# Squared-ReLU attention and an h-swish MLP in one kernel: the order of the loads in the first chunk, the queue of the weight loads, and the pace of the MLP's first units

## The chip, the cores and the metric

One core of one Trainium2 chip runs the whole kernel. The metric is the device time of one execution in microseconds, median of several runs; lower is better. A profiled execution gives the trace that is read below.

## The reference

`u`, `v` have shape 4 x 3008 x 256, `z` has 4 x 3008 x 64, all fp32. `w_in` (256 x 2048) and `w_out` (2048 x 256) arrive as float64.

```python
scores = (1.0 / S) * np.matmul(z, z.transpose(0, 2, 1))
attn = np.maximum(scores, 0.0) ** 2
x = (u * np.matmul(attn, v)).reshape(B * S, D)
h = x @ w_in
g = h * np.clip(h + 3.0, 0.0, 6.0) / 6.0
y = g @ w_out
```

## The kernel before

**Precision.** TensorE works on a rounded fp32 format (`F32R`). Each operand is split in a high part (rounded copy) and a low part (raw minus high, on VectorE), and a product is three matmuls: low x high, high x low, high x high. The scores need two, because `zx` and `zy` hold high and low of z stacked on the 128 partitions.

**Tiling.** The 24 chunks `(b, c)` are 512 rows of one batch entry b (the sixth of each has 448). For each chunk the attention walks 12 pairs p of 128 keys each: `scores(b, c, p)` makes 4 matmuls into PSUM, ScalarE takes the ReLU (`rt`), squares it into the rounded `ah` and once more into `r`, VectorE subtracts to get `al`; `attend(b, c, p)` then makes 12 matmuls of `ah`, `al` with `vh`, `vl`. The score matrix is symmetric: a pair computed in one chunk is written to DRAM (`keep`, tile `d`, two DMAs) and fetched again for its mirror in a later chunk (`fetch_mirrored`, tile `l`, four DMAs), where VectorE transposes it (`turn`, tile `rm`) and splits it (`from_mirror`); such a mirrored pair needs no score matmuls. The step number g counts the 288 pairs; scores are made two pairs ahead of `attend` for g < 28, one ahead later.

**First chunk.** At step p of chunk 0 (`i == 0`) the program also splits the next pair of v (`split_v(0, p + 1)`) and on even p a z piece (`split_z(0, p // 2 + 2)`): everything of batch entry 0 is loaded and split while its first chunk runs. Score pair p needs z piece p // 2. Before, v is loaded twice: raw by SP's queue, and rounded (`vh`) by GpSimd's queue; z pieces 2 to 5 are also loaded twice.

**MLP.** It trails the attention: for each chunk 16 units, `up(q)` (12 matmuls into `h`, then ScalarE and VectorE make `gh`, `gl`) and `down(q)` (12 matmuls into `y`). `mlp_units` emits as many units after each step as a target asks, from step FIRST = 28 on.

**Weights.** The float64 weights come in 16 pieces of 512 KB (`wraw`). `weight_ops` is a generator that turns them into fp32 high and low parts with 8 VectorE instructions each (`split64` six, `finish64` two) and one ScalarE copy; `weight_work(n)` emits the next n of these 128 instructions. Its first call only fetches two pieces; each later piece is fetched after the sixth instruction of the piece two before it. Unit n of the first MLP chunk needs piece n, and `weight_needed` emits what is missing on the spot.

**Buffers.** The pool `rpool` has 5 buffers with one tag, shared by `rt`, `r`, `rm`, `y` and `wraw` (two pieces of which are held while weights are under work). Each engine works through its instructions in program order, and so does each DMA queue's issuing engine: SP for most loads and stores, GpSimd (POOL) for the loads that round.

Of the kernel before, what the change touches and what calls it, by code (L numbers as in the profile page):

```python
# [13 lines left out]
B, S, D, DQK, DFF = 4, 3008, 256, 64, 2048  # L14
NT = B * S
P = 128
CH = 512
NCH = 6
NJ = 24
NPAIR = NJ // 2  # L20
# [2 lines left out]
NFP = NF // 2  # L23

FIRST = 28

TINY = 1.125 * 2.0 ** -15

# [2 lines left out]
def relu2_attention_then_hswish_mlp(  # L31
# [22 lines left out]
    nc = tc.nc  # L54
# [14 lines left out]
    def f(ap):  # L69
        return ap.bitcast(F32)  # L70
# [4 lines left out]
    def split(hi, lo, raw, rounded=False):  # L75
        if not rounded:
            nc.scalar.copy(out=hi, in_=raw)  # L77
        nc.vector.tensor_tensor(out=lo, in0=raw, in1=f(hi), op=ALU.subtract)  # L78
# [69 lines left out]
    def fetch_w(kind, q):  # L148
        _, _, src, cols = w_piece(kind, q)
        if wide:  # L150
            raw = rpool.tile([P, 2, D, 2], U32, tag="r", name="wraw")
            nc.sync.dma_start(
                out=raw.rearrange("p k n w -> p k (n w)"),
                in_=src[:, :, 2 * cols.start:2 * cols.stop],
            )
        else:
            raw = rpool.tile([P, 2, D], F32, tag="r", name="wraw")
            nc.sync.dma_start(out=raw, in_=src[:, :, cols])
        raws["w", kind, q] = raw

    raws = {}
# [3 lines left out]
    def fetch_v(b, p):  # L165

        if b == 0 and p < NPAIR - 1:
            raw = vpool.tile([P, 2, D], F32, tag="vl", name="vraw")
        else:
            raw = stg.tile([P, 2, D], F32, tag="stg", name="vraw")  # L170
        vh = vpool.tile([P, 2, D], F32R, tag="vh", name="vh")
        vt[b, p] = vh
        raws["v", p] = raw
        j0 = p * 2 * P
        for dst, queue in ((raw, nc.sync), (vh, nc.gpsimd))[:1 if b else 2]:
            if p < NPAIR - 1:
                queue.dma_start(
                    out=dst, in_=v[b, j0:j0 + 2 * P, :].rearrange("(r q) d -> q r d", q=P)
                )
            else:  # L180
                queue.dma_start(out=dst[:, 0, :], in_=v[b, j0:j0 + P, :])
                for h in range(2):
                    queue.dma_start(out=dst[64 * h:64 * h + 64, 1, :], in_=v[b, j0 + P:S, :])

    def split_v(b, p):
        vh, raw = vt[b, p], raws.pop(("v", p))
        vl = vpool.tile([P, 2, D], F32R, tag="vl", name="vl")
        split(vh, vl, raw, rounded=b == 0)
        vt[b, p] = (vh, vl)

    def fetch_z(b, k):
        if b == 0:
            raw = xpool.tile([P, CH], F32, tag=("xh0", "xh1", "xl0", "xl1")[k % 4], name="zraw")
        else:
            raw = stg.tile([P, CH], F32, tag="stg", name="zraw")
        zx = zpool.tile([P, CH], F32R, tag="zx", name="zx")
        zy = zpool.tile([P, CH], F32R, tag="zy", name="zy")
        zt[b, k] = (zx, zy)
        raws["z", k] = raw
        cols = slice(k * CH, (k + 1) * CH)  # L200
        nc.sync.dma_start(out=raw, in_=zz[b, :, cols])
        if b == 0 and k > 1:
            nc.gpsimd.dma_start(out=zx[0:64], in_=zz[b, 0:64, cols])
            nc.gpsimd.dma_start(out=zy[64:128], in_=zz[b, 64:128, cols])
# [33 lines left out]
    def fetch_mirrored():  # L238

        while to_fetch and len(mirrored) < 2:  # L240
            b, c, p = to_fetch[0]
            if (b, p // 2, c) not in whole:
                return
            fetch_pair(*to_fetch.pop(0))
# [33 lines left out]
    def turn(b, c, p):  # L278

        if p // 2 >= c:  # L280
            return
        n = width(c)
        t = mirrored.pop((b, c, p))
        rn = rpool.tile([P, 2, CH], F32, tag="r", name="rm")[:, :, :n]
        nc.vector.transpose(  # L285
            out=rn.rearrange("p r (k e) -> p r k e", e=32),
            in_=t[:, :n // 32].rearrange("p k (r e) -> p r k e", r=2),
        )
        turned[b, c, p] = rn
        fetch_mirrored()  # L290

    def from_mirror(b, c, p):
        n = width(c)
# [74 lines left out]
    def width(c):  # L368
        return CH if c < NCH - 1 else S - CH * (NCH - 1)
# [23 lines left out]
    def load_u(b, c):  # L393
        n = width(c)
        t0 = b * S + c * CH
        t = upool.tile([P, 2, CH], F32, tag="u", name="u")
        nc.sync.dma_start(
            out=t[:, :, :n], in_=ut[:, t0:t0 + n].rearrange("(k p) t -> p k t", p=P)
        )
        raw_x[b, c] = t  # L400
# [69 lines left out]
    chunks = [(b, c) for b in range(B) for c in range(NCH)]  # L470
    pairs = [(b, c, p) for b, c in chunks for p in pairs_of(c)]
# [4 lines left out]
    NU = len(units)  # L476
# [57 lines left out]
    def weight_work(n):  # L534
        for _ in range(n):
            next(w_ops, None)
# [17 lines left out]
    def maybe_split():  # L554

        if to_split and to_split[0] < avs[0]:
            i = to_split.pop(0)
            split_x(*chunks[i])
            if i + 2 < len(chunks):
                load_u(*chunks[i + 2])  # L560
# [9 lines left out]
    def turn_next():  # L570

        while g_turned[0] < min(g_done + 1, len(pairs)):
            turn(*pairs[g_turned[0]])
            g_turned[0] += 1

    with tc.manual_schedule():
        nc.vector.memset(three, 3.0)
        fetch_z(0, 0)
        fetch_v(0, 0)
        split_z(0, 0)  # L580
        fetch_z(0, 1)
        fetch_v(0, 1)
        weight_work(1)
        split_v(0, 0)
        split_z(0, 1)
        scores(0, 0, 0)
        fetch_z(0, 2)
        fetch_v(0, 2)
        scores(0, 0, 1)
        fetch_v(0, 3)  # L590
        g_done = 2
        to_fetch += [(b, c, p) for b, c, p in pairs if p // 2 < c]
        g_turned = [2]
        for i, (b, c) in enumerate(chunks):
            ahead = b + 1 if c == NCH - 1 and b + 1 < B else None
            for p in range(NPAIR):
                g = i * NPAIR + p
                pair = pairs[g]
                lead = 2 if g < FIRST else 1
                if i == 0:  # L600
                    if p + 1 < NPAIR:
                        split_v(0, p + 1)
                    if p % 2 == 0 and p // 2 + 2 < NCH:
                        split_z(0, p // 2 + 2)
                while g_done < min(g + lead + 1, len(pairs)):
                    scores(*pairs[g_done], square_on_act=i < 3)
                    g_done += 1
                if p > 3:
                    fetch_mirrored()
                if p < NPAIR - 1:  # L610
                    turn_next()
                if i == 0:
                    if p + 4 < NPAIR:
                        fetch_v(0, p + 4)
                    if p % 2 == 0 and p // 2 + 3 < NCH:
                        fetch_z(0, p // 2 + 3)
                    if p == 6:
                        load_u(*chunks[0])
                        load_u(*chunks[1])
                maybe_split()  # L620
                if g >= FIRST:
                    weight_work(5)
                elif p < NPAIR - 2:
                    weight_work(4 if i else 2)
                if ahead and p < NPAIR - 1:
                    if p:
                        split_v(ahead, p - 1)
                    if p < NPAIR - 2:
                        fetch_v(ahead, p)
                    if p % 2 == 1:  # L630
                        fetch_z(ahead, p // 2)
                    elif p:
                        split_z(ahead, p // 2 - 1)
                elif b and c == 0 and p < 4:
                    if p in (1, 2):
                        split_v(b, NPAIR - 3 + p)
                    if p < 2:
                        fetch_v(b, NPAIR - 2 + p)
                    if p == 2:
                        fetch_z(b, NCH - 1)  # L640
                    if p == 3:
                        split_z(b, NCH - 1)
                attend(*pair)
                turn_next()
                if p == NPAIR - 1:
                    avs[0] += 1
                total = len(pairs) - FIRST
                target = max(0, g + 1 - FIRST) * ((len(chunks) - 1) * NU - 4) // total
                mlp_units(target - units_done[0])
        mlp_units(1)  # L650
        maybe_split()
        mlp_units(len(chunks) * NU - units_done[0])
# [35 lines left out]
```

## Time and profile before

| | |
|---|---|
| median of 3 runs | 1992.83 us (1990.3 to 1993.12) |
| profiled execution, its own time | 1995.22 us |
| its span, first to last instruction | 1993.4 us |
| TensorE busy / VectorE / ScalarE / GpSimd | 1957.0 / 1278.8 / 987.6 / 14.2 us |
| granted TensorE clock, mean | 0.995 |
| matmuls | 8688 |

How to read it: busy TensorE time is the sum of stretches in which a matmul is in flight, so it does not tell apart a matmul at 2.4 GHz and one at 1.2 GHz; start-to-start distances and the granted clock do. PE is TensorE, PEld its weight loads, DVE VectorE, ACT ScalarE, POOL GpSimd, SP the queue engine. Times in the rows are microseconds from the span's start.

### The profile page before, as it was taken

How to read it: one execution, taken by the hardware profiler on the slowest of the kernel's cores; microseconds unless marked ns; L12 is line 12 of the kernel's file. 1: busy time of each engine (PE TensorE's matmuls, PEld its weight loads, DVE VectorE, ACT ScalarE, POOL GpSimd, SP SyncE). 2: the span in 40 equal slices, each digit the busy share in tenths (PEclk: the TensorE clock that was granted, in tenths of full speed). 3: DMA queues.
4: the chain of work that ended last, by engine and by line, in shares of the span. 5: the costliest groups of instructions: out<-in, count | busy, mean ns of one | idle time of the engine just before them, and what ended most of it. 6: DMA issues, size and time to landing. Idle time of an engine off the chain costs nothing.

```text
span 1993.4 us, 22057 instructions
## 1 busy us (share of the span) xinstructions
PE 1957.0 (98%) x8688; PEld 1634.6 (82%) x8688; DVE 1278.8 (64%) x1276; ACT 987.6 (50%) x1058; POOL 14.2 (1%) x26
## 2 busy tenths in 40 slices
PE   7899999999999999999999999999999999999999
PEld 5778788788888888888888888888888888888888
DVE  5798665676556666577655665657756555666654
ACT  6665444455544444456554454444554444444343
POOL 2000000000000000000000000000000000000000
PEclk9899999999999999999999999999999999999999
DMA  9753432525232233252323233334342323333300
GB/s 262 209 158 93 93 64 72 129 57 127 61 84 71 63 91 85 61 130 79 102 68 102 51 82 74 83 70 112 87 117 57 96 48 87 74 82 71 94 10 21
DMA packets 403272, 178.15 MB, mean 89 GB/s; under 512 B 250080, under 2 KB 385248, under 8 KB 403168
## 3 DMA queue, kind: packets, MB, share of 16 engines
q1 hardware_dynamic: 399232, 172.55, 34.3%
q0 software_dynamic: 3936, 4.20, 0.9%
q8 instruction: 68, 1.11, 0.2%
q14 instruction: 36, 0.29, 0.1%
HBM read 104.07 MB, written 72.61 MB: 89 GB/s over the span
## 4 chain that ended last, share of the span: by engine, by line
PE 88%; DVE 5%; ACT 2%; DMA 2%; issue 1%; SPq 1%; DVEq 0%; ACTq 0%
PE o L73 33%; PE h L73 24%; PE y L73 24%; PE s L73 7%; DMA zraw<-in_zz_dram 1%; DMA vraw<-in_v_dram 1%; DVE rt L436 1%; DVE al L354 1%; ACT rt L435 1%; DVE gl L78 1%; DVE al L301 1%; DVE rm L285 1%; ACT gh L77 0%; ACT rt L334 0%; ACT r L344 0%
## 5 line engine op out<-in xcount | busy, mean ns | idle before, releaser
L436 DVE SCALAR_TENSOR_TENSOR rt<-rt,h 128x1024 f32<-128x1024 f32 (+1 forms) x192 | 230.0, 1198 | 425.3 <-ACT rt L435 425.0
L435 ACT ACTIVATE rt<-h,three 128x1024 f32<-128x1024 f32 (+1 forms) x192 | 211.0, 1099 | 547.8 <-PE h L73 534.4
L73 PE MATMUL o<-ah,vl 128*128 128x512 f32 (+1 forms) x1152 | 447.3, 388 | 7.9 <-DVE u L405 2.7
L73 PE MATMUL o<-ah,vh 128*128 128x512 f32 (+1 forms) x1152 | 446.1, 387 | 0.0
L73 PE MATMUL o<-al,vh 128*128 128x512 f32 (+1 forms) x1104 | 429.2, 389 | 8.0 <-DVE al L301 5.8
L73 PE MATMUL y<-gh,w_out_l 128*128 128x512 f32 (+1 forms) x768 | 296.1, 386 | 1.6 <-DVE w_out_l L133 1.6
L73 PE MATMUL y<-gl,w_out_h 128*128 128x512 f32 (+1 forms) x768 | 296.4, 386 | 1.0 <-DVE gl L78 1.0
L73 PE MATMUL h<-xh,w_in_l 128*128 128x512 f32 (+1 forms) x768 | 295.9, 385 | 0.0
L73 PE MATMUL y<-gh,w_out_h 128*128 128x512 f32 (+1 forms) x768 | 295.9, 385 | 0.0
L73 PE MATMUL h<-xl,w_in_h 128*128 128x512 f32 (+1 forms) x768 | 295.9, 385 | 0.0
L73 PE MATMUL h<-xh,w_in_h 128*128 128x512 f32 (+1 forms) x768 | 295.9, 385 | 0.0
L78 DVE TENSOR_TENSOR gl<-rt,gh 128x1024 fp32r<-128x1024 f32 (+1 forms) x192 | 230.7, 1201 | 80.4 <-ACT gh L77 77.8
L73 PEld LDWEIGHTS o<-ah,vl 128*128 128x128 f32 x1152 | 217.6, 189 | 54.4 <-issue 4.5
L77 ACT CAST gh<-rt 128x1024 fp32r<-128x1024 f32 (+1 forms) x192 | 197.2, 1027 | 121.0 <-DVE rt L436 121.0
L73 PEld LDWEIGHTS o<-al,vh 128*128 128x128 f32 x1104 | 208.8, 189 | 52.1 <-DVE al L301 9.0
L73 PEld LDWEIGHTS o<-ah,vh 128*128 128x128 f32 x1152 | 217.8, 189 | 40.6
L334 ACT ACTIVATE rt<-s 128x1024 f32<-128x1024 f32 x168 | 171.2, 1019 | 115.5 <-PE s L73 108.9
L346 DVE TENSOR_TENSOR r<-rt 128x1024 f32<-128x1024 f32 (+1 forms) x139 | 168.8, 1214 | 87.0 <-ACT rt L334 86.8
L354 DVE TENSOR_TENSOR al<-r,ah 128x1024 fp32r<-128x1024 f32 (+1 forms) x139 | 169.7, 1221 | 18.5 <-ACT r L344 5.6
L301 DVE TENSOR_TENSOR al<-rm,ah 128x1024 fp32r<-128x1024 f32 (+1 forms) x120 | 141.2, 1176 | 42.4 <-ACT ah L299 42.3
L73 PEld LDWEIGHTS y<-gh,w_out_l 128*128 128x128 f32 x768 | 144.3, 188 | 29.3 <-DVE w_out_l L133 1.3
L73 PEld LDWEIGHTS y<-gl,w_out_h 128*128 128x128 f32 x768 | 144.2, 188 | 29.2 <-DVE gl L78 2.4
(51 smaller groups left out, 1809.5 us busy)
## 6 DMA issues: line engine op xcount, KB each, us to landing
d<-r SPq DMA_DIRECT2D x220, 256.0 KB, 2.9
l<-d SPq DMA_DIRECT2D x320, 128.0 KB, 3.2
l<-d SPq DMA_DIRECT2D x160, 112.0 KB, 2.9
vraw<-in_v_dram SPq DMA_DIRECT2D x44, 256.0 KB, 3.5
u<-in_ut_dram SPq DMA_DIRECT2D x20, 512.0 KB, 4.2
out_dram<-y SPq DMA_DIRECT2D x40, 256.0 KB, 3.5
zraw<-in_zz_dram SPq DMA_DIRECT2D x24, 256.0 KB, 3.8
wraw<-in_w_in_dram SPq DMA_DIRECT2D x8, 512.0 KB, 5.0
```

The lines of the kernel that those rows point to most:

```text
L73: nc.tensor.matmul(out, lhsT=lhsT, rhs=rhs, start=start, stop=stop)
L77: nc.scalar.copy(out=hi, in_=raw)
L78: nc.vector.tensor_tensor(out=lo, in0=raw, in1=f(hi), op=ALU.subtract)
L285: nc.vector.transpose(out=rn.rearrange("p r (k e) -> p r k e", e=32), in_=t[:, :n // 32].rearrange("p k (r e) -> p r k e", r=2),)
L301: nc.vector.tensor_tensor(out=al[:, :, :n], in0=rn, in1=f(ah[:, :, :n]), op=ALU.subtract)
L334: nc.scalar.activation(out=rn, in_=s[:, :, :n], func=AF.Relu, scale=1.0 / S)
L346: nc.vector.tensor_tensor(out=r2_of, in0=r_of, in1=r_of, op=ALU.mult)
L354: nc.vector.tensor_tensor(out=l_of, in0=r2_of, in1=h_of, op=ALU.subtract)
L435: nc.scalar.activation(out=rn, in_=h, func=AF.Relu, bias=three)
L436: nc.vector.scalar_tensor_tensor(out=rn, in0=rn, scalar=6.0, in1=h, op0=ALU.min, op1=ALU.mult)
```

## The change

Five edits. (1) The start loads z pieces 0 to 3 and v pairs 0 to 3 first; the first two weight pieces are no longer fetched there. In the loop, the loads of step p come at its beginning. (2) v of batch entry 0 is loaded once, raw; the rounded copy `vh` is made by ScalarE in `split_v`. (3) Weight pieces are fetched through GpSimd's queue, and weight work begins at step p = 5 of chunk 0. (4) Mirrored pairs are first fetched at p = 10 of chunk 0 (before: p = 4), and `u` at p = 7 (before: 6). (5) Weight instructions per step are 2 for p = 5 to 11 of chunk 0 (before: 2 for p = 0 to 9); then 4 in a step whose newest scores are direct and 2 (3 from g = 28) in one whose newest pair is mirrored (before: 4 in steps 0 to 9 of a chunk, 5 from g = 28); and the first SLOW = 16 units are emitted one per step (before: 364 units spread evenly over 260 steps, 1.4 each); the rest then run at 348 / 244 = 1.43 per step.

```diff
@@ fetch_w
-            nc.sync.dma_start(
+            nc.gpsimd.dma_start(
                 out=raw.rearrange("p k n w -> p k (n w)"),
...
@@ fetch_v
-        for dst, queue in ((raw, nc.sync), (vh, nc.gpsimd))[:1 if b else 2]:
...
+        if p < NPAIR - 1:
+            nc.sync.dma_start(
+                out=raw, in_=v[b, j0:j0 + 2 * P, :].rearrange("(r q) d -> q r d", q=P)
+            )
...
@@ split_v
-        split(vh, vl, raw, rounded=b == 0)
+        split(vh, vl, raw)
@@ before the loop
         fetch_z(0, 1)
         fetch_v(0, 1)
-        weight_work(1)
+        fetch_z(0, 2)
+        fetch_z(0, 3)
+        fetch_v(0, 2)
+        fetch_v(0, 3)
         split_v(0, 0)
         split_z(0, 1)
         scores(0, 0, 0)
-        fetch_z(0, 2)
-        fetch_v(0, 2)
         scores(0, 0, 1)
-        fetch_v(0, 3)
@@ in the loop
                 if i == 0:
+                    if p + 4 < NPAIR:
+                        fetch_v(0, p + 4)
+                    if p < 2:
+                        fetch_z(0, p + 4)
...
-                if p > 3:
+                if i or p > 9:
                     fetch_mirrored()
                 if p < NPAIR - 1:
                     turn_next()
+                if i == 0 and p == 7:
+                    load_u(*chunks[0])
+                    load_u(*chunks[1])
+                maybe_split()
                 if i == 0:
-                    if p + 4 < NPAIR:
-                        fetch_v(0, p + 4)
-                    if p % 2 == 0 and p // 2 + 3 < NCH:
-                        fetch_z(0, p // 2 + 3)
-                    if p == 6:
-                        load_u(*chunks[0])
-                        load_u(*chunks[1])
-                maybe_split()
-                if g >= FIRST:
-                    weight_work(5)
-                elif p < NPAIR - 2:
-                    weight_work(4 if i else 2)
+                    weight_work(2 if p > 4 else 0)
+                elif is_mirrored(*pairs[g_done - 1]):
+                    weight_work(3 if g >= FIRST else 2)
+                else:
+                    weight_work(4)
...
-                total = len(pairs) - FIRST
-                target = max(0, g + 1 - FIRST) * ((len(chunks) - 1) * NU - 4) // total
+                target = g + 1 - FIRST
+                if target > SLOW:
+                    all_but = (len(chunks) - 1) * NU - 4 - SLOW
+                    target = SLOW + (target - SLOW) * all_but // (len(pairs) - FIRST - SLOW)
                 mlp_units(target - units_done[0])
```

`is_mirrored(b, c, p)` returns `p // 2 < c`.

## Rows read from the trace of the kernel before

**Rows 1.** The page: busy time of the engines (us, share of the span, instructions), and the granted TensorE clock in 40 slices of 50 us.

```profile
PE 1957.0 (98%) x8688; PEld 1634.6 (82%) x8688; DVE 1278.8 (64%) x1276; ACT 987.6 (50%) x1058; POOL 14.2 (1%) x26
...
PEclk9899999999999999999999999999999999999999
```

**Rows 2.** What TensorE waited for in the first 260 us: total us, times, longest.

```profile
PE s L73 <- issue: 8.1, 2, 4.3
PE s L73 <- DVE zx L78: 6.4, 2, 6.1
PE o L73 <- DVE al L301: 3.6, 4, 1.4
PE o L73 <- DVE al L354: 2.2, 4, 0.9
PE y L73 <- DVE w_out_l L133: 1.6, 2, 0.9
```

**Rows 3.** Timeline of TensorE: the matmuls at which it had been idle in the two large gaps (start, duration, what, idle before).

```profile
30.52 0.47 PE L73 MATMUL s<-zy,zx 128*128 128x512 f32 x1 [3.82 <-issue]
33.49 0.77 PE L73 MATMUL o<-ah,vl 128*128 128x512 f32 x1 [1.49 <-DVE vl L78]
...
53.71 0.77 PE L73 MATMUL s<-zy,zx 128*128 128x512 f32 x1 [4.25 <-issue]
56.94 0.77 PE L73 MATMUL o<-ah,vl 128*128 128x512 f32 x1 [1.18 <-ACT rt L334]
```

**Rows 4.** The chain that ended last, 0 to 70 us: start, us, what.

```profile
17.87 11.06 DMA zraw<-in_zz_dram
...
33.49 5.08 PE o L73 x12
38.58 0.91 PE s L73 x4
39.49 2.72 PE o L73 x12
...
53.71 2.06 PE s L73 x4
...
56.94 5.28 PE o L73 x12
```

**Rows 5.** Timeline of SP's queue and of VectorE around the two gaps.

```profile
38.98 7.71 SPq L254 DMA_DIRECT2D l<-d  x8
...
47.27 0.47 SPq L201 DMA_DIRECT2D zraw<-in_zz_dram  x1
...
29.02 0.68 DVE L78 TENSOR_TENSOR zy<-zraw,zx 64x512 fp32r<-64x512 f32 x1 [6.24 <-DMA zraw<-in_zz_dram]
...
52.21 0.68 DVE L78 TENSOR_TENSOR zy<-zraw,zx 64x512 fp32r<-64x512 f32 x1 [6.69 <-DMA zraw<-in_zz_dram]
```

**Rows 6.** Stretches of 10 us: busy us (instructions) of each engine, granted TensorE clock, DMA share, GB/s.

```profile
20.00:30.00 10.00, 6.63 (x29) 5.18 (x28) 3.69 (x6) 3.66 (x4) 3.62 (x6) 1.00 1.25 342
30.00:40.00 10.00, 7.99 (x23) 5.92 (x24) 8.40 (x12) 6.42 (x7) 0.00 (x0) 0.66 0.70 189
50.00:60.00 10.00, 5.10 (x11) 3.68 (x12) 7.66 (x11) 4.09 (x4) 0.00 (x0) 0.58 1.08 358
```

**Rows 7.** DMA issues of the first 70 us: what, count, KB each, median us from issue to landing.

```profile
d<-r SPq DMA_DIRECT2D x19, 256.0 KB, 5.4
vraw<-in_v_dram SPq DMA_DIRECT2D x11, 256.0 KB, 5.6
vh<-in_v_dram POOLq DMA_DIRECT2D x11, 256.0 KB, 8.3
wraw<-in_w_in_dram SPq DMA_DIRECT2D x3, 512.0 KB, 9.7
```

**Rows 8.** The tile `wraw`, 0 to 250 us (16 pieces): landing times of its DMAs.

```profile
DMA to landing us min/median/max: 4.0/4.8/11.2
```

**Rows 9.** Timeline of ScalarE, one step of chunk 0 and a copy of 128x512.

```profile
33.71 1.04 ACT L344 ACTIVATE r<-rt 128x1024 f32<-128x1024 f32 x1
34.66 1.00 ACT L334 ACTIVATE rt<-s 128x1024 f32<-128x1024 f32 x1
35.69 1.06 ACT L343 ACTIVATE ah<-rt 128x1024 fp32r<-128x1024 f32 x1
...
27.47 0.60 ACT L117 CAST w_in_h<-t 128x512 fp32r<-128x512 f32 x1
```

**Rows 10.** VectorE's groups in the first 250 us, by shape: busy us, mean ns of one. Of the eight instructions of a weight piece the first and the last are shown (L101 to L133: 128 in all).

```profile
L354 DVE TENSOR_TENSOR al<-r,ah 128x1024 fp32r<-128x1024 f32 x26 | 31.8, 1223 | 6.3 <-ACT r L344 5.6
L285 DVE STREAM_TRANSPOSE rm<-l 128x1024 f32<-128x1024 f32 x12 | 14.9, 1238 | 0.0
L436 DVE SCALAR_TENSOR_TENSOR rt<-rt,h 128x1024 f32<-128x1024 f32 x12 | 14.5, 1212 | 5.8 <-ACT rt L435 5.8
L101 DVE TENSOR_SCALAR t<-wraw 128x512 uint32<-128x512 uint32 x16 | 6.7, 421 | 0.0
...
L133 DVE TENSOR_TENSOR w_in_l<-t,w_in_l 128x512 fp32r<-128x512 f32 x8 | 5.5, 691 | 0.2
```

**Rows 11.** Timeline of GpSimd and VectorE: a GpSimd DMA issue while VectorE is in a two-input instruction, and one just after it had waited.

```profile
11.58 0.73 POOL L177 DMA_DIRECT2D vh<-in_v_dram  x1 [0.16 <-issue]
...
11.44 1.23 DVE L354 TENSOR_TENSOR al<-r,ah 128x1024 fp32r<-128x1024 f32 x1
```

More of the change, by code (lines that the diff above doesn't have):

```diff
@@ L25 @@
 FIRST = 28
+SLOW = 16
 TINY = 1.125 * 2.0 ** -15
@@ L157, in fetch_w @@
             raw = rpool.tile([P, 2, D], F32, tag="r", name="wraw")
-            nc.sync.dma_start(out=raw, in_=src[:, :, cols])
+            nc.gpsimd.dma_start(out=raw, in_=src[:, :, cols])
         raws["w", kind, q] = raw
@@ L174, in fetch_v @@
         j0 = p * 2 * P
-        for dst, queue in ((raw, nc.sync), (vh, nc.gpsimd))[:1 if b else 2]:
[L176 to L183, printed above, removed]
+        if p < NPAIR - 1:
[3 more added lines that the diff above has]
+        else:
+            nc.sync.dma_start(out=raw[:, 0, :], in_=v[b, j0:j0 + P, :])
+            for h in range(2):
+                nc.sync.dma_start(out=raw[64 * h:64 * h + 64, 1, :], in_=v[b, j0 + P:S, :])
     def split_v(b, p):
@@ L290, in turn, with is_mirrored @@
         fetch_mirrored()
+    def is_mirrored(b, c, p):
+        return p // 2 < c
     def from_mirror(b, c, p):
@@ L611, in relu2_attention_then_hswish_mlp @@
                     turn_next()
+                if i == 0 and p == 7:
+                    load_u(*chunks[0])
+                    load_u(*chunks[1])
+                maybe_split()
                 if i == 0:
-                    if p + 4 < NPAIR:
-                        fetch_v(0, p + 4)
-                    if p % 2 == 0 and p // 2 + 3 < NCH:
-                        fetch_z(0, p // 2 + 3)
-                    if p == 6:
-                        load_u(*chunks[0])
-                        load_u(*chunks[1])
-                maybe_split()
-                if g >= FIRST:
-                    weight_work(5)
-                elif p < NPAIR - 2:
-                    weight_work(4 if i else 2)
+                    weight_work(2 if p > 4 else 0)
+                elif is_mirrored(*pairs[g_done - 1]):
+                    weight_work(3 if g >= FIRST else 2)
+                else:
+                    weight_work(4)
                 if ahead and p < NPAIR - 1:
```

## The prediction

> **What bounds the kernel now.** I read the page first, then TensorE's waits, the timeline at its two largest gaps, the chain that ended last, and VectorE's and ScalarE's groups. The page says that TensorE is the bound: 1957.0 of 1993.4 us busy, the clock full but for the second slice [rows 1]. No change that leaves the 8688 matmuls as they are can win more than TensorE's idle and slow-clock time, so I add up where that lies. In the first 260 us it waits some 25 us; the largest items are two waits for `s` put down to "issue" (8.1 us), the start itself (nearly all of the 6.4 behind `zx`), `al` (3.6 and 2.2) and `w_out_l` (1.6) [rows 2]. The change touches only this stretch; beyond it the code that is emitted is the same with the MLP a few units later.
>
> The two waits for `s` are the z pieces 4 and 5. TensorE stands still for 3.82 us before 30.52 and 4.25 us before 53.71 [rows 3], and VectorE, which splits z, had stood still for 6.24 and 6.69 us until `zraw` landed, at 29.02 and 52.21 [rows 5]. The first load took 11.06 us [rows 4] while the DMA engines moved 342 GB/s [rows 6]; the second was issued only at 47.27, because SP had spent 7.71 us from 38.98 on eight `l` fetches [rows 5]. So one is late by traffic and one by its place in SP's queue.
>
> What a gap costs is more than its idle time. After each the granted clock falls, to 0.66 in 30 to 40 us and 0.58 in 50 to 60 us [rows 6], that is for part of these stretches at the lower level of 1.2 GHz. Twelve `o` matmuls take 2.72 us at full clock, but 5.08 and 5.28 after the gaps; four `s` take 0.91, and 2.06 after the second [rows 4].
>
> **Part 1: z and v first.** Idle: 3.82 + 1.49 + 4.25 + 1.18 = 10.74 us [rows 3]. Slow clock: (5.08 - 2.72) + (5.28 - 2.72) + (2.06 - 0.91) = 6.1 us, and four `s` after the first gap, priced like those of the second, 1.1 more: 7.2 [rows 4]. Together 17.9 us to win. Unstalled, a step of chunk 0 is 16 matmuls of 0.227 us (2.72 / 12), 3.63 us; step 0 begins when `al` of pair 0 is there, at 11.44 + 1.23 = 12.7 us [rows 11], so step 4 near 27, step 5 near 31, step 7 near 38. Afterwards z pieces 4 and 5 are asked for in steps 0 and 1 and split in steps 4 and 6: some 15 us of room against landings of 5.4 to 11.06 us [rows 4, 7]. GpSimd's queue, which carried twelve loads of `vh` at 8.3 us each [rows 7], then holds only z at the start. The `l` fetch moves to step 10, behind the last z and v. I take the whole 17.9; below it the bound is 9 (one gap replaced by a new one), above it 18.5, since the first z and v loads meet less traffic too (at most some 0.6 us of the start).
>
> **Part 2: `vh` by ScalarE.** One copy of 128x512 takes 0.60 us. A step's `ah`, `r`, `rt` follow each other at some 1 us: 1.00 + 1.06 + 1.04 = 3.10 at most [rows 9]. So ScalarE needs 3.70 us per step against TensorE's 3.63, and 0.15 more from step 5 with one weight copy in four steps. Over twelve steps that is 0.07 x 12 + 0.15 x 7 = 1.9 us of backlog at worst, and scores lead by two steps, which hides some 3 us. I take 0.5; bounds 0 and 1.9. If the lead is already used up, the whole comes through.
>
> **Part 3: weights through GpSimd's queue, from step 5.** The issues leave SP (16 of some 0.5 us, hidden on SP as SP's 7.7 us of `l` are not, so nothing is taken for them). New: the first VectorE instruction on a weight now stands directly behind the fetch in the program, in step 5, and everything of VectorE behind it waits: `vl` of pair 7 first, then `al` of pair 8. GpSimd runs ahead, but its fetch needs a buffer of `rpool`, last held by an `r` whose store `d` takes 5.4 us to land [rows 7]. From near the start of step 5 (31 us) the fetch then needs 4.8 to 9.7 us [rows 7, 8], so it lands at 36 to 41 us; VectorE reaches the instruction near 35 (31, ScalarE's 3.1 for pair 7, `al` 1.2), and `vl` is needed in step 7, at 38. TensorE loses 0 to 4 us, with a drop of the clock at the top end, worth another 3. I take 2.0. From there two of five `rpool` buffers are held, as before, and `rt` can wait for `d` to land again: 0 to 2, I take 1.0. Later fetches are asked for ten weight instructions ahead: at 4 per step 2.5 x 3.63 = 9 us, against a median landing of 4.8 us [rows 8]: hidden.
>
> The Trainium skill, in "GPSIMD Engine Reference" (Specifications and Key points), says that GpSimd shares its SBUF interfaces with VectorE, with contention where VectorE has two SBUF inputs, as nearly all of its instructions here do. The issue at 11.58 took 0.73 us while the two-input `al` ran from 11.44 for its usual 1.23 [rows 10, 11]: neither was stretched. By the row the issues cost nothing; by the rule each might hold VectorE for its length, which is the port rival below.
>
> **Part 4: weight instructions where there is room.** 128 of them, from 0.42 to 0.69 us; the sixteen-fold groups add to 75.2 us, 0.59 us each, of which the first and the last are shown [rows 10]. A direct step of chunk 1: VectorE 1.22 + 4 x 0.59 = 3.58 against TensorE 3.63, as before. A mirrored step (no score matmuls, 2.72 us): before 1.24 + 1.22 + 4 x 0.59 = 4.82, after 3.64. Four such steps lie before g = 28, 4 x 1.18 = 4.7 us. The `al` waits are eight, 5.8 us, 0.73 each [rows 2]; I count one to the start, one to the MLP's first units and six, 4.4 us, to this part, which is then the most that is to be won. I take 3.0; bounds 0 and 4.4.
>
> **Part 5: one unit per step.** From g = 28, per step, before: VectorE 2.46 (attention) + 0.7 x 2.43 (half a unit is an `up`: 1.21 and 1.22) + 5 x 0.59 = 7.1 us, against TensorE's (12 + 16.8) x 0.227 = 6.5 in a mirrored step. After: 2.46 + 1.22 + 3 x 0.59 = 5.45 against 24 x 0.227 = 5.45 mirrored, 6.0 against 6.35 direct. So VectorE no longer falls behind. The weights: 14 + 44 + 12 = 70 instructions are emitted before g = 28 (before 77), then 3.5 per step; unit n needs 8n + 15 of them, which overtakes 70 + 3.5(n + 1) at n = 13: some 7 are emitted in a hurry for the last units. To win: `w_out_l` 1.6 and one `al` of 0.7 [rows 2], 2.3 us, and what the engine needs to run full again after each. I take 2.0; bounds -1 and 3. The units held back (six) are made up for at 1.43 per step; their matmuls are the same, so nothing is lost at the end.
>
> **Sum.** 17.9 - 0.5 - 2.0 - 1.0 + 3.0 + 2.0 = 19.4, with 0.4 for the start 19.8 us. Against the profiled execution's own 1995.22 that gives 1975.4; the median of the runs shown is 2.4 lower, 1992.83, and gives **1973.0**.
>
> **Rivals.**
> *A. A new wait in step 5.* The two gaps go, but VectorE's wait for the first weight piece stops TensorE for 4 us and drops the clock, like the old gaps (about 9 us each by Part 1); parts 4 and 5 bring half. For it: fetches took 9.7 us in the first 70 us [rows 7]. Against: that was at 342 GB/s, and afterwards there is no second load of v. 17.9 - 9 - 1.5 + 2.5 = 10 us: 1983.
> *B. Everything comes.* No wait in step 5, all of `al` and `w_out_l` won: 18.5 + 4.4 + 3 = 26 us: 1967.
> *C. The port.* Each of 16 issues of 0.73 us holds VectorE, 12 us in all, where VectorE sets the pace: 19.8 - 12 = 8: 1985. Against it: the issue and the `al` of the same moment [rows 11].
> *D. Slower.* Weight pieces come late through GpSimd's queue every time. VectorE then waits L - 9 us for each of five or six pieces in chunk 1 and L - 4 for the first, L being the time from request to landing. At L = 9.7 the loss is 10 us; it passes 20 and decides from L of about 11.5. Four pieces later, in the MLP, the spacing is 2.9 steps of 5.9 us, so no more is lost. For it: loads on that queue took 8.3 us for half the bytes [rows 7], and one weight piece took 11.2 [rows 8]. Against: both in the crowded first 30 us. At L = 13: 9 + 22 = 31 against 20, 2004.
> *E. No effect:* z is late again because eight loads at the start share the same engines. They have until step 2, 20 us, for 2 MB of raw loads and 0.5 MB of rounded z; even at the 189 GB/s of the slower stretch [rows 6] that is 13. I see nothing that speaks for it.
>
> **Chances.** Forecast (15 to 25 us won) 0.60; A 0.19; B 0.09; C 0.05; D 0.04; E 0.03. Range: up to A and C (1985) and just past B (1965) leaves out D, E and the tails. A change of 0.2%, 4 us, is about what a measurement of this kernel tells from none: faster 0.93, within it 0.03, slower 0.04.
>
> **What would show it.** In the profile after: no wait of `s` of more than 1 us in the first 60 us and a full granted clock from 10 us on (Part 1); the first `o` of chunk 1 near 57 us (12 steps of 3.63 after 12.7, 56.3); a VectorE idle time in front of the first L101 (step 5, near 35 us), and whether TensorE stands still 3 us later (A); `wraw` landing in 4 to 9 us with no idle of VectorE behind it (D); GpSimd's issues at 0.73 us (C); `al` waits under 2 us in 60 to 140, `w_out_l` waits gone (4, 5). The prediction is wrong if a gap of TensorE longer than 3 us stands anywhere in the first 60 us after the start.

## The result: 1.2% slower, and the profile after

The changed kernel takes 2015.59 us (median of 4, 2013.36 to 2018.43) against 1992.69 for the kernel before (1990.30 to 1993.12): ratio 1.0115, 95% interval 1.0103 to 1.0127. The forecast was 1973.0. The profiled execution took 2018.43 us, its span 2016.2. The page after, engines and clock:

```profile
PE 1964.3 (97%) x8688; PEld 1639.0 (81%) x8688; DVE 1279.4 (63%) x1276; ACT 993.8 (49%) x1070; POOL 16.2 (1%) x28
...
PEclk9999899999999999999999999999999999999999
```

Matmuls and VectorE's instructions are the same in number as in [rows 1]; only ScalarE's twelve copies and GpSimd's loads differ. So the 23 us are waiting and slow clock. TensorE's waits in the first 240 us of the kernel after (total us, times, longest), to be held against [rows 2]:

```profile
PE y L75 <- DVE w_out_l L135: 8.8, 1, 8.8
...
PE o L75 <- DVE al L358: 6.0, 5, 1.8
PE h L75 <- DVE w_in_l L135: 3.0, 1, 3.0
PE o L75 <- DVE u L409: 2.7, 1, 2.7
PE o L75 <- DVE vl L80: 2.6, 1, 2.6
PE o L75 <- DVE al L305: 1.4, 3, 0.8
```

The 8.1 us of `s` behind "issue" are gone. A wait of 8.8 us for weights is the largest new item. Timeline of TensorE, the matmuls in front of which it had been idle longest:

```profile
40.91 0.50 PE L75 MATMUL o<-ah,vl 128*128 128x512 f32 x1 [2.60 <-DVE vl L80]
...
113.23 0.50 PE L75 MATMUL o<-al,vh 128*128 128x512 f32 x1 [1.85 <-DVE al L358]
118.79 0.49 PE L75 MATMUL o<-ah,vl 128*128 128x512 f32 x1 [1.17 <-ACT ah L303]
...
178.38 0.57 PE L75 MATMUL o<-ah,vl 128*128 128x512 f32 x1 [2.71 <-DVE u L409]
...
214.96 0.47 PE L75 MATMUL h<-xh,w_in_l 128*128 128x512 f32 x1 [3.00 <-DVE w_in_l L135]
...
232.01 0.79 PE L75 MATMUL y<-gh,w_out_l 128*128 128x512 f32 x1 [8.85 <-DVE w_out_l L135]
```

Start times of steps can't be compared directly, since the changed kernel does fewer MLP units by a given step. I therefore use **lost time**: the start of a step's first `o` matmul, less the matmuls issued before it at 0.2267 us each (0.1985 for the chunks of 448 columns), the full-clock distances in the traces. It holds idle time and slow clock alike. From one profile of each kernel, in us, by stretch (steps g):

| kernel | to 12 | 12 to 28 | 28 to 47 | 47 to 287 |
|---|---|---|---|---|
| before | 27.7 | 4.2 | 6.3 | 18.9 |
| after | 14.5 | 14.6 | 20.7 | 30.7 |
| pace_only | 26.1 | 4.7 | 9.0 | 24.8 |
| five | 12.2 | 14.4 | 5.4 | 28.7 |
| early_fetch | 13.5 | 12.1 | 17.9 | 28.3 |
| vh_pool | 17.8 | 14.3 | 20.8 | 26.3 |
| late_copy | 12.3 | 13.1 | 5.7 | 29.5 |
| own_buf32 | 9.7 | 12.5 | 7.1 | 26.1 |
| catch_up | 28.4 | 4.2 | 8.0 | 18.0 |
| loads_only | 13.0 | 16.4 | 4.8 | 20.1 |
| both | 9.5 | 10.7 | 8.1 | 27.2 |
| combo_old | 9.5 | 11.2 | 3.5 | 24.9 |
| combo_catch | 9.4 | 9.9 | 8.0 | 25.3 |
| ahead | 26.7 | 4.6 | 6.2 | 20.3 |
| five_gap | 11.6 | 8.7 | 6.2 | 27.7 |
| best | 11.6 | 6.7 | 6.3 | 22.4 |

After minus before: -13.2, +10.4, +14.4, +11.8, together +23.4 against 22.9 of the medians. The first chunk wins what it should, nearly; three later stretches each give about as much away. Each line is one execution. `after`, `five`, `loads_only` and `five_gap` are one program up to step 12, and yet their first column differs by up to 2.9 us, so less than that means nothing there; in the second column programs that are the same up to step 28 differ by 0.8 at most. The profiled execution can also lie some us off the median: that of `five_gap` took 1992.06 us, the median of its ten is 1996.52.

### The profile page after: what moved, and what is told of

Same layout as the page of the kernel before. It is cut to its first block, busy times and chain, and to the rows that moved or that the text cites. A ratio compares the mean times of both kernels' runs of the same rounds, so it can differ in the third digit from the quotient of the medians.

```text
span 2016.2 us, 22065 instructions
## 1 busy us (share of the span) xinstructions
PE 1964.3 (97%) x8688; PEld 1639.0 (81%) x8688; DVE 1279.4 (63%) x1276; ACT 993.8 (49%) x1070; POOL 16.2 (1%) x28
## 4 chain that ended last, share of the span: by engine, by line
PE 85%; DVE 6%; ACT 4%; DMA 3%; issue 2%; SPq 1%; DVEq 0%; ACTq 0%; POOLq 0%
PE o L75 31%; PE h L75 24%; PE y L75 23%; PE s L75 6%; DMA zraw<-in_zz_dram 1%; ACT rt L439 1%; DVE rt L440 1%; SPq L255 1%; DVE al L358 1%; DMA vraw<-in_v_dram 1%; ACT gh L79 1%; DVE rm L286 1%; DVE gl L80 1%; ACT rt L338 1%; DVE al L305 1%
## 5 line engine op out<-in xcount | busy, mean ns | idle before, releaser
L75 PEld LDWEIGHTS h<-xh,w_in_l 128*128 128x128 f32 x768 | 144.5, 188 | 33.5 <-issue 3.4
```

The lines of the kernel that those rows point to most:

```text
L75: nc.tensor.matmul(out, lhsT=lhsT, rhs=rhs, start=start, stop=stop)
```

## The experiments

**Is it the weights at units 13 and 14, or the units held back?** Timeline of VectorE and ScalarE of the kernel after, around the two largest waits:

```profile
214.12 0.69 DVE L135 TENSOR_TENSOR w_in_l<-t,w_in_l 128x512 fp32r<-128x512 f32 x1
214.73 0.42 DVE L103 TENSOR_SCALAR t<-wraw 128x512 uint32<-128x512 uint32 x1
220.62 1.22 DVE L440 SCALAR_TENSOR_TENSOR rt<-rt,h 128x1024 f32<-128x1024 f32 x1 [5.47 <-ACT rt L439]
...
227.57 0.68 DVE L108 SCALAR_TENSOR_TENSOR t<-wraw,t 128x512 uint32<-128x512 uint32 x1
...
231.26 0.69 DVE L135 TENSOR_TENSOR w_out_l<-t,w_out_l 128x512 fp32r<-128x512 f32 x1
...
219.47 1.12 ACT L439 ACTIVATE rt<-h,three 128x1024 f32<-128x1024 f32 x1 [7.66 <-PE h L75]
```

This is one serial chain. TensorE waits for `w_in_l` until 214.8, computes `h` of unit 13, ScalarE takes it at 219.47, and VectorE, idle for 5.47 us, goes on with what stands behind that unit in its order: `rt`, `r`, `gl`, `al`, `rm`, `xl`. Only then come seven weight instructions up to the one that TensorE waits for, until 232.01. Counted in the program, unit 13's last two weight instructions are emitted in its own step, and of these seven four are the next step's regular ones; three are emitted on the spot because unit 14 lacks them.

`five`, against the kernel after:

```diff
+                elif g >= FIRST:
+                    weight_work(5)
                 elif is_mirrored(*pairs[g_done - 1]):
-                    weight_work(3 if g >= FIRST else 2)
+                    weight_work(2)
```

> The changed kernel with 5 weight instructions in every step from g = 28 on. Theory F expects the two waits at units 13 and 14 (3.0 and 8.8 us idle, with the slow clock some 13 to 16 us) to vanish and no wait of more than 1 us in their place: about 2002. If VectorE is short of time there anyway (my own Part 5), the waits move to al and the time stays within 4 us of 2015.6. Theory S expects the loss after 250 us to stay as it is.

Measured: 1999.96 us, 1.0042 (1.0027 to 1.0057) of before. Both waits are gone; 28 to 47 falls from 20.7 to 5.4. In 125 to 240 us one wait is left:

```profile
PE o L75 <- DVE u L409: 3.1, 1, 3.1
```

It stands at the end of chunk 2, at 176.88 us, and the kernel after has it too (2.71 us at 178.38): there, too, weight instructions stand in VectorE's order, in front of the product with `u`. The kernel before waits 0.5 us for `u` up to 240 us. So weights that come late cost 15 us, and VectorE was not short of time there.

`pace_only`, the pace put into the kernel before:

```diff
-                target = max(0, g + 1 - FIRST) * ((len(chunks) - 1) * NU - 4) // total
+                target = g + 1 - FIRST
+                if target > 16:
+                    all_but = (len(chunks) - 1) * NU - 4 - 16
+                    target = 16 + (target - 16) * all_but // (total - 16)
```

> The kernel before with one edit: the first 16 MLP units one per step, the rest at 1.43 per step. Theory F (weights run short: in the changed kernel units 13 and 14 find their weight instructions not yet emitted, which are then placed behind the units' own work) expects no loss here, since 5 weight instructions per step stay: within 3 us of 1992.7. Theory S (six units held back change how MLP and attention interleave at every later batch start, worth the 10 us that the changed kernel loses after 250 us) expects about 2003, with waits like those near 887 and 1410 us of the changed kernel.

Measured: 2001.93 us, 1.0053 (1.0036 to 1.0070): the pace alone costs some 10 us, of which the profile shows 2.7 in steps 28 to 47 and 5.9 later. `catch_up` keeps the 16 slow units and then takes two per step until back on the old line:

```diff
+                late_by = g + 1 - FIRST
+                target = min(target, late_by if late_by <= 16 else 16 + 2 * (late_by - 16))
```

> The kernel before with the first 16 units one per step and then two per step until the count is back on the kernel before's line (near step 57). If it is the six units still held back at later batch starts that cost 'pace_only' 7 to 10 us, nearly all of it comes back: 1992 to 1995. If any other interleaving costs as much, about 2001.

Measured: 1994.48 us, 1.0015 (1.0005 to 1.0024), and 18.0 late. Three quarters of the loss come back (7.5 us between the medians), so the units still held back cost it, not the 16 slow steps. `ahead` shifts the units the other way:

```diff
+                if g >= 56:
+                    target = min(target + 4, (len(chunks) - 1) * NU - 4)
```

> The kernel before with the MLP four units ahead of its line from step 56 on. If being behind is what cost 'pace_only' 7 to 10 us, being ahead costs nothing or gains a little: 1988 to 1993. If any shift of the units against the attention's batch starts costs, 1996 to 2002.

Measured: 1995.78 us, 1.0016 (1.0007 to 1.0026), between the two expectations. A shift of the units either way costs something, the one behind more. The kernel after shows where. These are waits of TensorE from 240 us to the end; the kernel before has `al` 2.2, `ah` 2.2, `u` 2.2 and `gl` 1.0 there:

```profile
PE y L75 <- ACT gh L79: 3.7, 2, 3.0
PE o L75 <- DVE u L409: 3.2, 4, 0.9
PE o L75 <- DVE al L305: 2.8, 5, 1.0
...
PE h L75 <- ACT rt L338: 1.6, 1, 1.6
```

The longest, before 887 us, stands in chunk 11 (counted from 0), the last of batch entry 1, in which v and z of the next entry are loaded: ScalarE's `vh` copy there waits 6.30 us for a load of `vraw`, with the unit's `rt` behind it in its queue. Summed by chunk, chunk 11 and chunk 17, the last of batch entry 2, lose 14.7 us of lost time in the kernel after, 3.7 before, 12.0 in `pace_only`, 4.1 in `catch_up` and 9.4 in `ahead`. Why four units of shift bring such meetings about was not settled.

A smaller part has a source that I overlooked. I took the code beyond the first chunk for the same, but the new condition `i or p > 9` in place of `p > 3` also lets mirrored pairs be fetched in the first steps of every later batch entry, ahead of its last z piece. SP's queue and ScalarE at the start of batch entry 1 in `loads_only` (an experiment below, with the pace of before), and then SP's queue in the kernel before:

```profile
455.39 5.05 SPq L255 DMA_DIRECT2D l<-d  x8
460.49 0.61 SPq L202 DMA_DIRECT2D zraw<-in_zz_dram  x1
...
465.23 0.62 ACT L79 CAST zx<-zraw 64x512 fp32r<-64x512 f32 x1 [6.65 <-DMA zraw<-in_zz_dram]
```

```profile
459.33 0.64 SPq L201 DMA_DIRECT2D zraw<-in_zz_dram  x1
...
474.74 4.61 SPq L254 DMA_DIRECT2D l<-d  x8
```

A unit's `rt` stands behind these copies of z, and TensorE then waits 1.77 us. Chunks 6 and 18, the first of batch entries 1 and 3, together lose 0.6 us before and at most 0.9 in the three runs that keep the old condition (`pace_only`, `catch_up`, `ahead`); with the new one it is 2.5 in the kernel after, 2.4 or more in all the others, and 4.7 in `loads_only` and `best`. No run undoes this condition alone, so its price is only read from traces.

**The first chunk.** The kernel after, GpSimd and VectorE:

```profile
31.87 1.49 POOL L154 DMA_DIRECT2D wraw<-in_w_in_dram  x2 [26.28 <-DMA vraw<-in_v_dram]
...
34.20 1.23 DVE L358 TENSOR_TENSOR al<-r,ah 128x1024 fp32r<-128x1024 f32 x1 [1.66 <-ACT r L348]
39.83 0.43 DVE L103 TENSOR_SCALAR t<-wraw 128x512 uint32<-128x512 uint32 x1 [4.40 <-DMA wraw<-in_w_in_dram]
40.17 0.69 DVE L80 TENSOR_TENSOR vl<-vraw,vh 128x512 fp32r<-128x512 f32 x1
```

`early_fetch` and `vh_pool`:

```diff
-                    weight_work(2 if p > 4 else 0)
+                    weight_work(2 if p > 4 else 1 if p == 2 else 0)
```

> The changed kernel with the first two weight pieces fetched in step 2 instead of step 5; the first weight instruction stays in step 5. Both theories on the first chunk expect the 2.6 us wait for vl near 41 us and the slow clock behind it, 4.5 us together, to go. Theory L (the stall eats the two-pair lead, and steps 12 to 28 lose 10 us because no lead is left) expects half or more of those 10 us to go too: 2003 to 2008. If steps 12 to 28 are slow for another reason, 2011, with the same 10 us there.

Measured: 2009.92 us, 1.0088 (1.0073 to 1.0103). The first weight instruction no longer waits, but `vl` still stops TensorE, one step earlier (2.2 us): the two buffers are fetched into from 20.7 us on, ScalarE's `rt` waits 4.1 us for a buffer whose store must land, and `r` comes late instead. Of the lost time only 1.0 goes up to step 12, 2.5 in 12 to 28. The wait was moved and not removed, so this run does not decide on theory L; `own_buf32` below, without any such wait, does.

```diff
-        split(vh, vl, raw)
+        split(vh, vl, raw, rounded=b == 0)
```

(with the loads of `fetch_v` as before the change)

> The changed kernel with vh loaded by GpSimd's queue as before, in place of ScalarE's twelve copies of 0.6 us. If ScalarE's full first chunk (3.7 us of work in steps of 3.63 us) is what leaves no lead for steps 12 to 28, 5 to 10 us come back: 2006 to 2011. If not, no gain, and the 3 MB more of loads delay the first weight piece: 2015 to 2020.

Measured: 2016.99 us, 1.0130 (1.0115 to 1.0145): no gain. The first chunk loses 3.3 us more, and steps 12 to 28 are as slow. ScalarE's copies are not what makes those steps slow.

**Steps 12 to 28.** `loads_only` undoes Parts 4 and 5, except that the old condition `p < NPAIR - 2` (no weight instructions in the last two steps of a chunk) stays out:

```diff
-                elif is_mirrored(*pairs[g_done - 1]):
-                    weight_work(3 if g >= FIRST else 2)
                 else:
-                    weight_work(4)
+                    weight_work(5 if g >= FIRST else 4)
...
+                target = max(0, g + 1 - FIRST) * ((len(chunks) - 1) * NU - 4) // total
```

> The changed kernel with Parts 4 and 5 undone: 4 weight instructions per step in chunks 1 and 2 and 5 from g = 28, mirrored or not, and the MLP at 1.4 units per step as before. The first chunk's 13 us should stay won up to step 12. Theory P expects steps 12 to 28 to be as slow as in the changed kernel or slower (every second step then has the copy in the bad place), so 10 us go there. With the pace of before no loss after 250 us: 1988 to 1993. If the whole loss came from Parts 4 and 5, 1977 to 1980.

Measured: 1993.62 us, 1.0009 (0.9999 to 1.0018). Most of the later loss is gone, 14.7 us are won by step 12, and 12.2 given back by step 28. So those 16 steps are a cause by themselves. In the kernel after, ScalarE and VectorE around step 25:

```profile
107.28 0.62 ACT L119 CAST w_out_h<-t 128x512 fp32r<-128x512 f32 x1 [2.21 <-DVE t L116]
108.72 1.03 ACT L338 ACTIVATE rt<-s 128x1024 f32<-128x1024 f32 x1 [0.81 <-DVE w_out_l L125]
...
111.95 1.23 DVE L358 TENSOR_TENSOR al<-rt,ah 128x1024 fp32r<-128x1024 f32 x1 [2.72 <-ACT rt L348]
...
115.22 1.28 DVE L409 TENSOR_TENSOR u<-u,o 128x512 f32<-128x512 f32 x2
116.42 1.24 DVE L286 STREAM_TRANSPOSE rm<-l 128x1024 f32<-128x1024 f32 x1
...
117.69 1.04 ACT L303 CAST ah<-rm 128x1024 fp32r<-128x1024 f32 x1 [5.77 <-DVE rm L286]
```

Three things are to be seen. The weight copy stands in ScalarE's queue in front of the next pair's `rt` and waits 2.21 us for VectorE. The `rt` behind it waits for a buffer that a weight piece held until its sixth instruction. And `rm` of pair 26 comes only after all of VectorE's weight instructions of steps 22 and 23. `late_copy` takes the first away, on `five`; the newest copies are left for the next scores:

```diff
-    def flush_copies():
-        while copies:
+    def flush_copies(keep=0):
+        while len(copies) > keep:
...
-        flush_copies()
+    def finish64(hi, lo, f0, keep):
+        flush_copies(keep)
...
+            yield from finish64(hi, lo, f0, len(begun))
```

> The kernel 'five' (changed kernel, 5 weight instructions per step from g = 28), in which finishing one weight piece no longer puts the ScalarE copy of the next piece into ScalarE's queue; that copy then follows the next pair's squares. Theory P (in the changed kernel the copy is queued between two pairs' ReLUs and waits there for VectorE, so that rt of the next pair, and with it al, come late in steps 19, 21, 23 and 25) expects the loss in steps 12 to 28 (14.4 us in 'five' against 4.2 before) to fall by 3 to 6 us: 1994 to 1997. If it is the buffers that weights and scores share, the loss stays within 1.5 us.

Measured: 1998.53 us, 1.0035 (1.0024 to 1.0046), which can't be told from `five`; 1.3 us less in 12 to 28. ScalarE's waits in 60 to 125 us, `five` and then `late_copy`, show why so little: the wait of the copy goes, those for the buffers grow.

```profile
ACT w_out_h L119 <- DVE t L116: 5.8, 2, 3.6
...
ACT rt L338 <- DVE w_out_l L125: 0.8, 1, 0.8
```

```profile
ACT rt L338 <- DVE w_out_l L125: 3.3, 1, 3.3
...
ACT rt L338 <- DVE w_in_l L125: 1.6, 1, 1.6
ACT r L348 <- DVE w_in_l L125: 1.4, 1, 1.4
```

`own_buf32` takes the second away, on `five`:

```diff
-    rpool = ctx.enter_context(tc.tile_pool(name="rpool", bufs=5))
+    rpool = ctx.enter_context(tc.tile_pool(name="rpool", bufs=3))
+    rawpool = ctx.enter_context(tc.tile_pool(name="rawpool", bufs=2))
...
-            raw = rpool.tile([P, 2, D, 2], U32, tag="r", name="wraw")
+            raw = rawpool.tile([P, 2, D, 2], U32, tag="w", name="wraw")
...
```

> The kernel 'five' with two buffers of their own for the weight pieces and three left for rt, r, rm and y (the same memory). Theory B (rt of pair 25 takes over a weight piece's buffer and waits for the sixth instruction on it, which stands in VectorE's queue) expects the 7.4 us lost in steps 24 to 26 to shrink to 1 to 3 and no wait of rt for a weight instruction. Theory P expects those steps unchanged. After step 45 only three buffers are left for the MLP, so the whole time may be longer; the steps up to 40 are what counts: step 40 begins at 202.0 us in 'five', 196 to 198 under B.

Measured: 1993.59 us, 1.0011 (1.0001 to 1.0020). The wait for the first weight piece is gone too (9.7 to step 12, and no wait of TensorE above 0.4 us in 10 to 60): it was the buffer that was late, though the row above names a load of `vraw` as what released the fetch. In 12 to 28 only 1.9 us are won, so theory L falls. From the start of step 24 to that of step 26 the lost time is 6.4 us, where I expected 1 to 3, and step 40 begins at 199.2 us, not at 196 to 198; the other wait stays, and grows against the 5.8 us of `five`:

```profile
ACT w_out_h L120 <- DVE t L117: 7.7, 3, 3.5
ACT w_in_h L120 <- DVE t L117: 2.2, 1, 2.2
```

`both` is `late_copy` and `own_buf32` together.

> 'late_copy' and 'own_buf32' together. In steps 16 to 28 'late_copy' still shows rt and r waiting for a weight piece's buffer (6.3 us), and 'own_buf32' shows the weight copy waiting in ScalarE's queue in front of rt (9.9 us): each cause alone is enough to make rt late. If so, taking away both brings what neither did: the loss in steps 12 to 28 falls from 12.5 us in 'own_buf32' to 5 to 8, and the time to 1986 to 1990. If VectorE's load alone sets these steps, no more than 1 us changes: 1993.

Measured: 1992.97 us, 1.0001 (0.9991 to 1.0010). Steps 24 to 26 fall from 7.4 us of lost time in `five` (6.4 in `own_buf32` and in `late_copy`) to 3.6, but 12 to 28 only to 10.7, and the time can't be told from that of `own_buf32`: half an answer. `five_gap` takes the third thing away alone, on `five`:

```diff
+                elif p > 9:
+                    pass
                 elif is_mirrored(*pairs[g_done - 1]):
```

> 'five' without weight instructions in the last two steps of a chunk before g = 28, as the kernel before has it (steps 22 and 23). The eight instructions of these steps (some 4.4 us of VectorE) stand in front of the product with u and of the transpose of pair 26, the first mirrored one of chunk 2, for which ScalarE and then TensorE wait 5.8 and 2.7 us. If that is the cause, the 7.4 us lost in steps 24 to 26 fall to 1 to 3 and the time to 1994 to 1997. If it is only the late rt of pair 25 (copy and buffer), they stay above 5.

Measured: 1996.52 us, 1.0018 (1.0008 to 1.0027), by the ratios 4.8 us under `five`. Steps 24 to 26 fall to 3.4, and 12 to 28 to 8.7. TensorE's waits in 90 to 125 us, `five` and then `five_gap`:

```profile
PE o L75 <- DVE al L358: 3.1, 2, 1.9
PE o L75 <- ACT ah L303: 1.3, 1, 1.3
PE o L75 <- DVE al L305: 1.1, 2, 0.8
```

```profile
PE o L75 <- DVE al L305: 2.0, 3, 0.9
PE o L75 <- DVE al L358: 1.9, 2, 1.3
PE o L75 <- ACT ah L303: 0.6, 1, 0.6
```

**Versions put together.** `combo_old` is `both` with the weight counts and the pace of `loads_only`; `combo_catch` is `both` with the pace of `catch_up`.

> 'both' with the weight instructions and the MLP's pace of the kernel before (4 per step in chunks 1 and 2, 5 from g = 28; 1.4 units per step). The first chunk's 15 us, kept through steps 12 to 28, and no loss after 250 us: step 28 begins at 114 to 118 us, and the time is 1974 to 1981. If four weight instructions in mirrored steps cost what 'loads_only' lost in steps 16 to 28 (16 us), 1988 to 1993.

Measured: 1985.81 us, 0.9965 (0.9953 to 0.9976), faster than before, between the two expectations; step 28 begins at 119.5 us, later than expected.

> 'both' with the pace of 'catch_up' (16 units one per step, then two per step until back on the line of before). 'both' less what the held-back units cost after 250 us (6 to 8 us): 1979 to 1984.

Measured: 1988.56 us, 0.9976 (0.9967 to 0.9985). That is 4.4 us under `both` and not 6 to 8. The late column falls by 1.9 only, from 27.2 to 25.3: with the pace loss moves from chunks 11 and 17 (8.8 to 5.0) to chunks 6 and 18 (2.5 to 5.4), where mirrored pairs are fetched early; the rest was not settled.

`best`, against `combo_old`:

```diff
-                    weight_work(2 if p > 4 else 0)
+                    weight_work(2 if p > 1 else p)
...
-                else:
-                    weight_work(5 if g >= FIRST else 4)
+                elif g >= FIRST:
+                    weight_work(5)
+                elif p < NPAIR - 2:
+                    weight_work(4)
```

> 'combo_old' without weight instructions in steps 22 and 23 and with the first weight work in step 2 of chunk 0 (fetch in step 1), so that as many are done by g = 28 as in the kernel before (77). 'combo_old' still lost 8.8 us in steps 24 to 28; if the instructions of steps 22 and 23 are the cause, 4 to 6 of them come back: 1979 to 1983. If the earlier weight work costs ScalarE its first chunk, step 12 begins later than 56.5 us and the time stays near 1985.

Measured: 1984.12 us, 0.9955 (0.9940 to 0.9969), the lowest median of this study, 8.8 us under the kernel before; its interval overlaps with that of `combo_old`. Something of both halves of the expectation shows: 12 to 28 falls to 6.7, and the first chunk gives 2.1 back (step 12 at 57.4 us), which is no more than that column's spread. The time lies just outside the 1979 to 1983 expected. Its page:

```profile
PE 1952.3 (98%) x8688; PEld 1629.4 (82%) x8688; DVE 1280.3 (65%) x1276; ACT 993.5 (50%) x1070; POOL 16.1 (1%) x28
...
PEclk9999999999999999999999999999999999999999
```

## Why the prediction was wrong, step by step

- **Part 1 was right.** Both waits for `s` and the slow clock behind them are gone; by step 6 the kernel after had lost 10.0 us, the kernel before 18.5, and by step 12 14.5 against 27.7. `own_buf32`, which has not the wait of Part 3, stands at 9.7 there, 18.0 under the kernel before, where this part took 17.9.
- **Part 2 was right:** `vh_pool`, which takes ScalarE's copies away again, wins nothing, and in `own_buf32`, which has them, TensorE waits for 0.4 us in all in 10 to 60 us; 0.5 were taken.
- **Part 3 was mis-sized.** The wait behind the first weight fetch is rival A's at half its price, with 2.60 us of idle time at 40.91 and 1.9 us of slow clock, 4.5 together; I took 2.0 and 1.0. The reason was the one named, a buffer of `rpool` (`own_buf32`). Up to step 12 the sum gave 14.8 us to win; 13.2 came.
- **Part 4 failed, -10.4 in place of +3.0.** It added up VectorE's instructions per step and compared sums. The waits that it aimed at did shrink, `al` of mirrored pairs from 3.6 to 1.4 us, but `al` of direct pairs rose from 2.2 to 6.0. What set these steps is the order in the queues of VectorE and ScalarE, and the shared buffers: the eight instructions that the old condition kept out of the last two steps of a chunk now stand before the transpose of pair 26 (`five_gap`: 5.7 us of the 10 by the profiles, 4.8 by the ratios). I had counted them as supply in Part 5 and not as a delay here. The copy's place in ScalarE's queue and the buffer that `rt` takes over account for another share: 3.7 us between `five` and `both`. Those two can stand in for each other, which shows in steps 24 to 26: 1.0 us for either edit alone, 3.8 for both; over the whole stretch 1.3 and 1.9 against 3.7 is too near to tell. The kernel before has the same copies and the same shared buffers, and loses 4.2 us in the stretch; why they cost more after the change was not settled.
- **Part 5 failed, -14.4 in place of +2.0.** Its own count was nearly right: the supply is just used up at n = 13 and three instructions short at unit 14, where it said some seven. The step that failed is that no term of the sum prices this. The late weights stand behind unit 13's own work, so TensorE waits for them through the chain `h`, `rt`, seven VectorE instructions and the weights: 3.0 + 8.85 us idle, and with 4.1 us of slow clock (the twelve `h` and twelve `y` took 4.43 and 5.14 us in place of 2.72) 16 in all; `five` takes 15.3 away.
- **"Nothing is lost at the end" failed, by 11.8 us.** That the matmuls are the same is true; the waits are not. 11.0 of the 11.8 stand in chunks 11 and 17. `pace_only` has 5.9 more than the kernel before in this column, 8.3 in these two chunks, and `catch_up` takes it away again: the held-back units cause most of it, but how stays open. "The code that is emitted is the same" was wrong as well: mirrored pairs are fetched earlier at every batch start, which costs some 2 us in the kernel after (chunks 6 and 18: 2.5 against 0.6), as far as the traces tell.
- **The rivals.** C did not happen: GpSimd's weight issues took 0.72 to 0.75 us each, and nine two-input instructions of 1024 columns that ran beside an issue took 1.22 to 1.23 us, as they do elsewhere. D neither: VectorE waited for a weight load once, 4.40 us, and loads landed in 3.8 to 8.5 us. The slower outcome came from places where I had no rival, since I looked for one only among the loads and their issues. The sign of being wrong that I had named, a gap of more than 3 us in the first 60 us, did not come either (2.60 us): it looked only where the gain was to come from.

## What to carry to other kernels

Where filler work is paced against the main work, check for each unit whether its input is emitted before it, and price a shortfall as the whole chain behind which it is queued, not as its own length. An engine's total per step says little when it stands close to its bound: here it was what stood directly in front of the instruction that the critical engine needed next, in an in-order queue or in a shared buffer pool, that decided. Two waits in the same place can hide each other, as in steps 24 to 26; take both away before calling either harmless. Where a condition is changed for the first chunk, read what it does in the later ones.

## What the runs showed of the hardware

After an idle time of 2.60 us TensorE's clock fell: the granted clock is 0.83 in 40 to 50 us, and the twelve `o` matmuls after the wait took 4.53 us in place of 2.72. I had expected a fall only at the top end of 0 to 4 us. The 1.85 us before 113.23 (with 0.45 us and one matmul ahead of them) were followed by one too (0.83 in 110 to 120 us), while the 2.21 us before 36.38 in `early_fetch` were not (1.00 in 30 to 40 and in 40 to 50 us), so the length of a wait alone did not tell. The rows, the last of them behind the 8.85 us wait:

```profile
40.00:50.00 10.00, 9.09 (x33) 7.35 (x34) 8.28 (x13) 7.04 (x9) 0.00 (x0) 0.83 0.65 183
...
110.00:120.00 10.00, 5.82 (x15) 3.55 (x14) 6.87 (x10) 4.17 (x5) 0.00 (x0) 0.83 0.13 31
...
230.00:240.00 10.00, 7.99 (x26) 6.42 (x27) 5.39 (x7) 1.04 (x2) 0.00 (x0) 0.67 0.47 109
```

These are stretches of the kernel after: length, busy us of TensorE, its weight loads, VectorE, ScalarE and GpSimd, then granted clock, DMA share and GB/s.

A GpSimd DMA issue did touch VectorE, though not where I looked. Its two-input instructions beside one took their usual time. But in the kernel after three of the four one-input instructions on a weight piece that ran beside an issue took 0.62 us, in place of 0.38 to 0.44 for all the others: about 0.6 us in the whole run, against the 12 of rival C. One of them in the kernel after:

```profile
95.53 0.72 POOL L154 DMA_DIRECT2D wraw<-in_w_in_dram  x1 [4.64 <-DVE al L305]
```

```profile
95.86 0.62 DVE L112 TENSOR_SCALAR wraw<-wraw 128x512 uint32<-128x512 uint32 x1
```
